# Linear attention feeding a mixture of experts: q and the decays turned by VectorE in 32x32 blocks, and the next unit's loads put inside the store step

## The chip, the cores and the metric

The kernel runs on one core of one Trainium2 chip. The metric is the time on the device in microseconds (us) from the first to the last instruction of an execution and what lies around it, as the median of several runs.

## The reference

Attention with a decaying state runs first; its output y, with the heads of a token side by side, is the input x of a mixture of 8 experts whose weights P come from a Sinkhorn iteration over the logits.

```
def _attn_ref(q, k, v, alpha):            # each (B=4, H=8, S=768, D=48), float32
    state = zeros((B, H, D, D))
    for t in range(S):
        state = alpha[:, :, t, :, None] * state + einsum('bhd,bhe->bhde', k[:, :, t], v[:, :, t])
        y[:, :, t] = einsum('bhd,bhde->bhe', q[:, :, t], state)
...
def _moe_ref(x, w_gate, w1, w2):          # x (3072, 384), w1 (8, 384, 1024), w2 (8, 1024, 384)
    logits = x @ w_gate
    P = exp(logits - logits.max())
    for _ in range(8):
        P /= P.sum(1, keepdims=True) + 1e-09
        P /= P.sum(0, keepdims=True) + 1e-09
        P *= N / E
    for e in range(E):
        out += P[:, e:e+1] * (maximum(x @ w1[e], 0) @ w2[e])
```

## The kernel before

The tokens are worked in twelve **units** of 256 tokens, three for each of the four batches, numbered 0 to 11 through all batches (`g`). A unit has two **chunks** of 128 tokens. Units 0 and 1 take another path (`direct_chunk`); units 2 to 11 go through three generators that an order written out by hand (`START`, then `UNIT` repeated for each unit) advances step by step, mixed with steps `f` that emit tiles of the first three experts. The order of the instructions on each engine is the order in which these steps emit them; nothing is reordered at run time.

- `attn_block` (steps `b`, sixteen for a unit) loads q, k and alpha of the unit as `qt`, `kt`, `al`, with 16 tokens of a head in each of 128 partitions, and multiplies decays into them and takes the products within 16 tokens: GpSimd makes the products `tmp`, VectorE sums them into the score table `AB`. The first `tmp` of a unit multiplies `qt` by `kt`. The three tiles have one buffer each, so that a unit's loads come after the stores of the unit before.
- The last step of `attn_block`, the **store step**, writes kt, qt, the block decays (`ds`) and the scores (`As`) to DRAM and reads them back in other layouts: `KN` and `QN` with a token in each partition and the heads beside each other, `DN` for the decays, `an` for the scores, `VN` for v straight from the input. For units from 3 on (`g >= TAB`) it also writes decays to `dsw` and reads them back as `win`. All are issued on SP's queue, in the order of the code.
- `attn_decays` (step `d`) turns `DN` with four transposes on TensorE (`psd`) and makes small tables of decays.
- `attn_chunk` (steps `c`) turns k and q of a chunk with four transposes each on TensorE (`psk`, `psq`); ScalarE copies them out of PSUM as `Tk` and `Tq`; VectorE multiplies decays in (`decq`, `deck`), GpSimd one of them (`deck`) and then `A`, which spreads `an` over a 128x128 mask. TensorE makes the scores (`psl`) and the output (`psy`), `attn_tail` adds the state.

Expert tiles write `ps` in PSUM, in four banks; ScalarE reads them as `h` (Relu) or as `r`, VectorE takes the low part of `h`, and a bank is free after that. `r` is stored to DRAM as `raw` on SP's queue.

Engines issue in order: an instruction that waits holds up all that stand behind it on its engine, and a DMA that waits holds up SP's queue.

Of the kernel before, what the change touches and what calls it, by code (L numbers as in the profile page):

```python
# [25 lines left out]
def tile_gla_moe(ctx: ExitStack, tc: tile.TileContext, q, k, v, alpha, wg, w1, w2, out):  # L26
# [126 lines left out]
    def quarter(j):  # L153
        return slice(32 * j, 32 * j + 32)
# [134 lines left out]
    KN = [ap1.tile([P, NCH, H, DP], F32, name=f"KN{i}") for i in range(2)]  # L289
    DN = [ap1.tile([16, H, DP], F32, name="DN")] * 2  # L290
    VW = DP + D
# [7 lines left out]

    for x in DN[:1] + ST:  # L300
        GE.memset(x, 0.0)
# [26 lines left out]
    for i in range(NLV):  # L328
        L = 1 << i

        r = sm.tile([P, 16], F32, tag="oddr", name=f"oddr_{i}")
        VE.tensor_reduce(r[:, :16 // L], same.rearrange("p (n z t) -> p n z t", z=2, t=L)[:, :, 0],
                         axis=AX.X, op=ALU.add)
        VE.tensor_copy(odd[:, i].rearrange("p (n t) -> p n t", t=L),
                       r[:, :16 // L].unsqueeze(2).to_broadcast([P, 16 // L, L]))

    def load_v(x, b, t0, Q=SP):
# [3 lines left out]
    def direct_chunk(ch, got):  # L341
# [140 lines left out]
        yield from attn_tail(0, ch, vn[:, c], K_, Q_, A, Dl[:, :, 0])  # L482

    def attn_block(b, u, got):

# [3 lines left out]
        vec = VE  # L489
        src = lambda x: x[b, :, t0:t0 + U].rearrange("h (n t) d -> n h (t d)", t=16)  # L490
        qt, kt, al = (ap1.tile([P, 16, D], F32, tag=x, name=f"{x}_{nm}") for x in ("qt", "kt", "al"))
        for x, y in ((qt, q), (al, alpha), (kt, k)):
            (GE if lop[0] else SP).dma_start(x, src(y))
        if TAB <= g < TAB + 2:
# [50 lines left out]
        if True:  # L545

            t = mult(pool, "tmp4", [16], Af[:, 0:256:17], qt, kt)
            yield
            total(*t)
            yield  # L550
            vec.tensor_mul(qt, qt, al)
            for L in (1, 2, 4, 8):
                todo, merge = level(L)
                for x in todo:
                    t = mult(pool if lop[0] else x[0], *x[1:])
                    yield
# [9 lines left out]
        As = dr.tile([H, U, 16], F32, tag="As", name=f"As_{nm}")  # L566
        qn, kn, dn = QN[g % 2], KN[g % 2], DN[g % 2]
        vn = VN[g % 2]
        an = ap2.tile([P, NCH, H, 16], F32, tag="an", name=f"an_{nm}")
        def put(t, t_):  # L570
            for x, y in ((ks, ko), (qs, qo)):
                dma(x[:, t:t_].rearrange("h (n t) d -> n h (t d)", t=16), y[t // 2:t_ // 2])

        put(0, U)
        dma(ds.rearrange("h n d -> n h d"), al[:, 0])
        for c in range(NCH) if g >= TAB else ():
            dma(dsw[g % 2][:, c, :8].rearrange("h n d -> n h d"), al[c * 64:c * 64 + 64, 0])
        if True:
            dma(As.rearrange("h (n s) t -> n h (s t)", s=16), Af)
        for c in range(NCH):  # L580
            sl = slice(c * P, (c + 1) * P)
            dma(kn[:, c, :, :D], ks[:, sl].rearrange("h t d -> t h d"))
            dma(qn[:, c, :, :D], qs[:, sl].rearrange("h t d -> t h d"))
            if c == 0:
                dma(dn[:, :, :D], ds.rearrange("h n d -> n h d"))
            dma(an[:, c], As[:, sl].rearrange("h p t -> p h t"))
            load_v(vn[:, c], b, t0 + c * P)
        if g >= TAB:
            win = ap1.tile([P, 7, D], F32, tag="tmp2", name=f"win_{nm}")
            for c in range(NCH):  # L590
                e = dsw[g % 2][0, c, 1]
                dma(win[c * 64:c * 64 + 64], bass.AP(tensor=e.tensor, offset=e.offset,
                                                     ap=[[D, 8], [NCH * 15 * D, H], [1, 7 * D]]))
            got["win"] = win
        got.update(qn=qn, kn=kn, dn=dn, vn=vn, an=an)
        yield

    def attn_decays(b, u, got):

        nm = f"{b}_{u}"  # L600
        dn = got["dn"]
        psd = psa.tile([P, 512], F32, tag="psa", name=f"psd_{nm}")
        for j in range(NP):
            tr(psd[:, j * 16:(j + 1) * 16], dn[:, 2 * j:2 * j + 2].rearrange("p h d -> p (h d)"), ident[:16, :16])
        dT = ap2.tile([P, NCH, NP, 2, 4], F32, tag="dT", name=f"dT_{nm}")
        VE.tensor_copy(dT.rearrange("p c j z n -> p c j (z n)"),
                              psd[:, :NP * 16].rearrange("p (j c n) -> p c j n", c=NCH, n=8))

# [32 lines left out]
    def attn_chunk(b, ch, got):  # L641
# [5 lines left out]
        nm = f"{b}_{ch}"  # L647
        T2 = []
        for s in "kq":
            ps = psa.tile([P, 512], F32, tag="psa", name=f"ps{s}_{nm}")  # L650
            for j in range(NP):
# [22 lines left out]
        for L, tq, tk in ((32, got["q32"][:, c].rearrange("p j z b -> p (j z) b"),  # L674
# [832 lines left out]
```

## Time and profile before

| | |
|---|---|
| time, median of 3 runs | 1646.62 us (1645.75 to 1653.32) |
| the profiled execution's own time | 1645.72 us |
| its span, first to last instruction | 1643.8 us |
| TensorE (PE) busy | 1591.0 us, 97% of the span |
| VectorE (DVE) busy | 1262.3 us, 77% |
| ScalarE (ACT) busy | 916.5 us, 56% |
| GpSimd (POOL) busy | 390.9 us, 24% |
| attention and first experts | to about 735 us |

An engine's busy time is the sum over its instructions; a row of a timeline gives the start, the busy time, the instructions merged in it, and in brackets the idle time before them with what ended it. PE is TensorE's matmuls, SPq SyncE's DMA queue.

### The profile page before, as it was taken

Reading aid. Unit: us, or ns where it says so; the run is one execution under the profiler, and the core shown is the slowest. Engines: PE = TensorE matmul, PEld = TensorE weight load, DVE = VectorE, ACT = ScalarE, POOL = GpSimd, SP = SyncE. Lnnn points to the kernel's source line nnn. Section 1 sums busy time; section 2 is a strip of 40 time slices with the busy share of each in tenths; the row PEclk is TensorE's granted clock in tenths of the full one; section 3 lists DMA queues with packets and bytes.
Section 4 is the critical chain, followed back from the end, with each engine's and each line's share of the span. In section 5 each row is a group of like instructions: output and inputs, shape, how many; then the busy total and the mean of one; then the engine's idle time right before and its main releaser. Section 6 shows DMA issues by size and latency. Waiting matters only on the chain.

```text
span 1643.8 us, 50626 instructions
## 1 busy us (share of the span) xinstructions
PE 1591.0 (97%) x21760; PEld 1399.8 (85%) x21760; DVE 1262.3 (77%) x2693; ACT 916.5 (56%) x2106; POOL 390.9 (24%) x395
## 2 busy tenths in 40 slices
PE   5689999999999999999999999999999999999998
PEld 4567777777777777777899999999999999999998
DVE  5887776665666565367798988898888888899998
ACT  3655533333333333355777766666666676765554
POOL 5457544643644462175000000000000000000000
PEclk9799999999999999999999999999999999999999
DMA  7463243144134323120412131213121322213332
GB/s 165 103 139 105 67 116 93 53 125 110 57 89 116 81 69 89 42 79 30 107 50 88 60 98 59 97 60 88 55 92 59 88 69 88 67 62 117 113 121 88
DMA packets 180072, 141.92 MB, mean 86 GB/s; under 512 B 112232, under 2 KB 169832, under 8 KB 179848
## 3 DMA queue, kind: packets, MB, share of 16 engines
q1 hardware_dynamic: 178104, 131.99, 29.0%
q0 software_dynamic: 1744, 6.70, 1.6%
q8 instruction: 170, 2.79, 0.7%
q14 instruction: 54, 0.44, 0.1%
HBM read 91.00 MB, written 47.65 MB: 84 GB/s over the span
## 4 chain that ended last, share of the span: by engine, by line
PE 87%; DVE 4%; DMA 1%; SPq 1%; ACT 1%; issue 1%; POOL 0%; DVEq 0%; ACTq 0%; POOLq 0%
PE ps L67 30%; PE p1a L67 17%; PE p2x L67 14%; PE p1b L67 10%; PE p2y L67 7%; PE p2v L67 4%; PE psl L67 2%; PE psy L67 2%; SPq L58 1%; DVE h L58 1%; DVE w L58 1%; PE psk L70 1%; DVE acc L58 1%; PE psq L70 1%; PE pss L67 0%
## 5 line engine op out<-in xcount | busy, mean ns | idle before, releaser
L67 PEld LDWEIGHTS <-h 128*128 128x128 f16 x6684 | 570.5, 98 | 105.2 <-issue 2.5
L67 PEld LDWEIGHTS <-w 128*128 128x128 f16 x6984 | 565.3, 98 | 58.1 <-issue 12.4
L67 PE MATMUL ps<-xT,w 128*128 128x256 f16 (+1 forms) x2664 | 301.2, 272 | 8.6 <-DVE h L58 6.4
L67 PE MATMUL ps<-w,h 128*128 128x384 f16 x1728 | 299.3, 326 | 0.8 <-DVE h L58 0.7
L58 DVE TENSOR_TENSOR h<-hf,h 128x256 f16<-128x256 f32 x472 | 279.0, 618 | 23.6 <-ACT h L58 23.6
L67 PE MATMUL p2x<-w,h 128*128 128x192 f16 x2820 | 270.7, 246 | 0.0
L58 ACT CAST h<-hf 128x256 f16<-128x256 f32 x472 | 249.5, 567 | 9.3 <-DVE hf L58 4.5
L58 DVE TENSOR_TENSOR hf<-hf 128x256 f32<-128x256 f32 x354 | 181.8, 513 | 39.6 <-ACT hf L58 31.2
L58 ACT ACTIVATE h<-ps 128x256 f16<-128x256 f32 (+1 forms) x296 | 110.5, 377 | 161.5 <-PE ps L67 160.3
L58 POOL TENSOR_TENSOR tmp<-qt,kt 128x768 f32<-128x768 f32 (+2 forms) x87 | 156.2, 1802 | 156.2 <-DVE qt L58 84.6
L58 DVE SCALAR_TENSOR_TENSOR h<-ps,h 128x256 f16<-128x256 f32 (+1 forms) x296 | 117.5, 413 | 96.0 <-ACT h L58 94.7
L67 PE MATMUL p1a<-xT,w 128*128 128x128 f16 (+1 forms) x2160 | 179.1, 237 | 0.0
L67 PE MATMUL p1b<-xT,w 128*128 128x256 f16 (+1 forms) x1440 | 158.0, 246 | 0.0
L58 ACT ACTIVATE hf<-p1b 128x512 f32<-128x512 f32 x118 | 70.3, 596 | 151.4 <-DVE h L58 118.4
L67 PEld LDWEIGHTS <-wx 128*128 128x128 f16 x2160 | 147.4, 98 | 7.9 <-issue 4.9
L67 PE MATMUL p2y<-w,h 128*128 128x192 f16 x1404 | 134.9, 246 | 0.0
L58 DVE TENSOR_REDUCE AB<-tmp 128x16 f32<-128x768 f32 (+2 forms) x90 | 81.4, 904 | 64.1 <-POOL tmp L58 63.7
L67 PE MATMUL p1a<-xc,wx 128*128 128x128 f16 x1440 | 119.5, 219 | 3.6 <-DVE p1b L58 1.6
L58 ACT ACTIVATE hf<-p1a 128x512 f32<-128x512 f32 x118 | 70.4, 597 | 64.7 <-PE p1a L67 64.7
L58 ACT COPY r<-ps 128x384 f32<-128x384 f32 x72 | 34.2, 476 | 102.3 <-PE ps L67 62.3
L58 ACT COPY A<-psl 16x128 f32<-16x128 f32 (+3 forms) x164 | 52.4, 326 | 49.2 <-PE psl L67 47.7
L67 PE MATMUL p2v<-w,h 128*128 128x192 f16 x708 | 68.1, 246 | 0.0
(235 smaller groups left out, 1830.5 us busy)
## 6 DMA issues: line engine op xcount, KB each, us to landing
accd<-acc SPq DMA_DIRECT2D x48, 384.0 KB
acc<-accd SPq DMA_DIRECT2D x48, 384.0 KB
raw<-r SPq DMA_DIRECT2D x72, 192.0 KB
ri<-raw SPq DMA_DIRECT2D x72, 192.0 KB
w1f<-in_moe_w_dram SPq DMA_DIRECT2D x20, 384.0 KB
w2f<-in_moe_w_dram SPq DMA_DIRECT2D x5, 1536.0 KB
VN<-in_v_dram SPq DMA_DIRECT2D x48, 96.0 KB
out_dram<-acc SPq DMA_DIRECT2D x11, 384.0 KB
```

The lines of the kernel that those rows point to most:

```text
L58: r = f(*a, **k_)
L67: tc.keep_in_program_order(nc.tensor.matmul(out_, lhsT, rhs, start=start, stop=stop, **k_))
L70: tc.keep_in_program_order(nc.tensor.transpose(out=out_, in_=in_, identity=idn))
```

## The change

Four things are changed, for the units from 3 on (`turned`); unit 2 keeps the old way, with `DN` in a buffer of `Tq`.

1. q and the decays go to DRAM with the even heads ahead of the odd ones, and come back as `QN` and `DY` in pieces: 32 tokens (or blocks) in 32 partitions, one 32-wide or 16-wide piece of a head's 48 numbers after the other, four DMAs each. VectorE's 32x32 block transpose then gives `Tq` and `dT` directly. The transposes `psq` and `psd` on TensorE and ScalarE's copy of `psq` are gone. k is turned on TensorE as it was.
2. `load_block(g + 1, SP)` loads q, k and alpha of the next unit inside the store step, behind the reads of DY, KN (first chunk) and QN, and ahead of win, an and the second chunk's KN. The first step of `attn_block` then finds them loaded. In units 4 and 5 these loads were issued on GpSimd's queue before.
3. Within the store step the decays are stored first, then k, q and the scores.
4. v is loaded behind: in the second step of `attn_block` where the buffer is free by then, and at the end of the store step otherwise.

```diff
+    DY = ap1.tile([P, NP * 16 // 32, 32], F32, name="DY")
...
+    def in32(x):
+        return x.rearrange("p c h d -> p (c h d)").rearrange("p (s t) -> p s t", t=32)
...
+    loaded = {}
+
+    def load_block(g, eng):
+
+        if g in loaded or g >= len(units):
+            return
+        b, u = units[g]
+        src = lambda x: x[b, :, u * U:(u + 1) * U].rearrange("h (n t) d -> n h (t d)", t=16)
+        loaded[g] = [ap1.tile([P, 16, D], F32, tag=x, name=f"{x}_{b}_{u}") for x in ("qt", "kt", "al")]
+        for x, y in zip(loaded[g], (q, k, alpha)):
+            eng.dma_start(x, src(y))
+
     def attn_block(b, u, got):
 
         g = b * NU + u
         t0 = u * U
         nm = f"{b}_{u}"
         vec = VE
-        src = lambda x: x[b, :, t0:t0 + U].rearrange("h (n t) d -> n h (t d)", t=16)
-        qt, kt, al = (ap1.tile([P, 16, D], F32, tag=x, name=f"{x}_{nm}") for x in ("qt", "kt", "al"))
-        for x, y in ((qt, q), (al, alpha), (kt, k)):
-            (GE if lop[0] else SP).dma_start(x, src(y))
+        load_block(g, GE if lop[0] else SP)
+        qt, kt, al = loaded[g]
+        turned = g >= TAB
+        vn = VN[g % 2]
...
             t = mult(pool, "tmp4", [16], Af[:, 0:256:17], qt, kt)
             yield
+            ahead = turned and all(steps[i] >= XDONE[i] for i in range((g - 2) * NCH, (g - 1) * NCH))
+            for c in range(NCH) if ahead else ():
+                load_v(vn[:, c], b, t0 + c * P)
             total(*t)
             yield
...
-        qn, kn, dn = QN[g % 2], KN[g % 2], DN[g % 2]
-        vn = VN[g % 2]
+        qn, kn = QN[g % 2], KN[g % 2]
         an = ap2.tile([P, NCH, H, 16], F32, tag="an", name=f"an_{nm}")
-        def put(t, t_):
-            for x, y in ((ks, ko), (qs, qo)):
-                dma(x[:, t:t_].rearrange("h (n t) d -> n h (t d)", t=16), y[t // 2:t_ // 2])
-
-        put(0, U)
-        dma(ds.rearrange("h n d -> n h d"), al[:, 0])
-        for c in range(NCH) if g >= TAB else ():
-            dma(dsw[g % 2][:, c, :8].rearrange("h n d -> n h d"), al[c * 64:c * 64 + 64, 0])
-        if True:
-            dma(As.rearrange("h (n s) t -> n h (s t)", s=16), Af)
-        for c in range(NCH):
-            sl = slice(c * P, (c + 1) * P)
-            dma(kn[:, c, :, :D], ks[:, sl].rearrange("h t d -> t h d"))
-            dma(qn[:, c, :, :D], qs[:, sl].rearrange("h t d -> t h d"))
-            if c == 0:
-                dma(dn[:, :, :D], ds.rearrange("h n d -> n h d"))
-            dma(an[:, c], As[:, sl].rearrange("h p t -> p h t"))
-            load_v(vn[:, c], b, t0 + c * P)
-        if g >= TAB:
-            win = ap1.tile([P, 7, D], F32, tag="tmp2", name=f"win_{nm}")
+        dsh = lambda: [dma(dsw[g % 2][:, c, :8].rearrange("h n d -> n h d"), al[c * 64:c * 64 + 64, 0])
+                       for c in range(NCH)]
+        load_an = lambda c: dma(an[:, c], As[:, c * P:(c + 1) * P].rearrange("h p t -> p h t"))
+        def load_win():
+
+            win = got["win"] = ap1.tile([P, 7, D], F32, tag="tmp2", name=f"win_{nm}")
             for c in range(NCH):
                 e = dsw[g % 2][0, c, 1]
                 dma(win[c * 64:c * 64 + 64], bass.AP(tensor=e.tensor, offset=e.offset,
                                                      ap=[[D, 8], [NCH * 15 * D, H], [1, 7 * D]]))
-            got["win"] = win
-        got.update(qn=qn, kn=kn, dn=dn, vn=vn, an=an)
+
+        if turned:
+            heads = lambda x, r: x.rearrange("(r j) t d -> r j t d", r=2)[r]
+            rows = lambda x, r: x.rearrange("(m r) t d -> r m t d", r=2)[r]
+            for r in range(2):
+                dma(heads(ds, r).rearrange("j n d -> n j d"), rows(al, r)[:, 0])
+            dsh()
+            dma(ks.rearrange("h (n t) d -> n h (t d)", t=16), ko)
+            for r in range(2):
+                dma(heads(qs, r).rearrange("j (n t) d -> n j (t d)", t=16), rows(qo, r))
+            dma(As.rearrange("h (n s) t -> n h (s t)", s=16), Af)
+            load_k = lambda c: dma(kn[:, c, :, :D], ks[:, c * P:(c + 1) * P].rearrange("h t d -> t h d"))
+            for x, y in ((DY, ds), (in32(qn), qs)):
+                for i in range(4):
+                    r, z = divmod(i, 2)
+                    w = 32 - 16 * z
+                    dma(x[quarter(i), :, :w], heads(y, r).rearrange("j t d -> (j t) d")
+                        .rearrange("(s t) d -> t s d", t=32)[:, :, 32 * z:32 * z + w])
+                if y is ds:
+                    load_k(0)
+            load_block(g + 1, SP)
+            load_win()
+            load_an(0)
+            load_k(1)
+            load_an(1)
...
+        for c in range(NCH) if turned and not ahead else ():
+            load_v(vn[:, c], b, t0 + c * P)
+        got.update(qn=qn, kn=kn, vn=vn, an=an)
...
-        dn = got["dn"]
-        psd = psa.tile([P, 512], F32, tag="psa", name=f"psd_{nm}")
-        for j in range(NP):
-            tr(psd[:, j * 16:(j + 1) * 16], dn[:, 2 * j:2 * j + 2].rearrange("p h d -> p (h d)"), ident[:16, :16])
+        dn = got.get("dn")
         dT = ap2.tile([P, NCH, NP, 2, 4], F32, tag="dT", name=f"dT_{nm}")
-        VE.tensor_copy(dT.rearrange("p c j z n -> p c j (z n)"),
-                              psd[:, :NP * 16].rearrange("p (j c n) -> p c j n", c=NCH, n=8))
+        if dn is None:
+            VE.transpose(dT.rearrange("p c j z n -> p j c (z n)"), DY.rearrange("p m (j c n) -> p (m j) c n", c=NCH, n=8))
...
+        tabbed = got["k128"] is None
         for s in "kq":
+            if tabbed and s == "q":
+                t = ap2.tile([P, NP, P], F32, tag=f"T{s}", name=f"T{s}_{nm}")
+                y = in32(got["qn"]).rearrange("p (j s) t -> p j (s t)", j=NP)
+                VE.transpose(t, y[:, :, c * P:(c + 1) * P])
+                T2.append(t)
+                continue
```

On SP's queue, the store step of unit 5 stood so before, from the read of the decays on (`DN`, `an` the scores, `VN` v, `win` the windows of decays, `qt`, `al`, `kt` the loads for unit 6, `raw` stores of expert tiles):

```order
L58 DMA DN_120<-ds_1_2_4576 16x8x48
L58 DMA an_1_2_4578<-As_1_2_4577 128x8x16
L58 DMA VN1_124<-in_v_dram 128x4x48 x2
L58 DMA KN1_119<-ks_1_2_4575 128x8x48
L58 DMA QN1_117<-qs_1_2_4574 128x8x48
...
L58 DMA win_1_2_4596<-dsw1_149 64x1x336 x2
L58 DMA qt_2_0_4599<-in_q_dram 128x1x768
L58 DMA al_2_0_4601<-in_alpha_dram 128x1x768
L58 DMA kt_2_0_4600<-in_k_dram 128x1x768
L58 DMA raw0_104<-r_0_6_4649 128x384
```

The same place in the changed kernel:

```order
L58 DMA KN1_119<-ks_1_2_4565 128x8x48
L58 DMA QN1_117<-qs_1_2_4564 32x32x32
L58 DMA QN1_117<-qs_1_2_4564 32x32x16
...
L58 DMA qt_2_0_4586<-in_q_dram 128x1x768
L58 DMA kt_2_0_4587<-in_k_dram 128x1x768
L58 DMA al_2_0_4588<-in_alpha_dram 128x1x768
L58 DMA win_1_2_4592<-dsw1_149 64x1x336 x2
L58 DMA an_1_2_4568<-As_1_2_4567 128x8x16
L58 DMA KN1_119<-ks_1_2_4565 128x8x48
L58 DMA an_1_2_4568<-As_1_2_4567 128x8x16
L58 DMA raw0_104<-r_0_6_4637 128x384
```

The loads for unit 6 moved ahead of `win`, of both halves of `an` and of the second chunk's `KN`; v is gone from the step.

On VectorE, unit 4's first chunk before (`dT` the turned decays, `AB` the sum over unit 5's first product `tmp`, `decq` and `deck` the products on the turned q and k):

```order
L58 COPY dT_1_1_3745<-psd_1_1_3740 128x64
L58 TENSOR_TENSOR e2_1_1_3747<-dT_1_1_3745 128x32
...
L58 TENSOR_REDUCE AB1_126<-tmp4_1_2_30_3738 128x16
L58 TENSOR_TENSOR decq32_1_2_3779<-Tq_1_2_3777,q32_0_133 128x256
L58 TENSOR_TENSOR deck32_1_2_3781<-Tk_1_2_3770,k32_0_135 128x256
L58 TENSOR_TENSOR decq64_1_2_3783<-Tq_1_2_3777,pre_0_129 128x256
```

and now:

```order
L58 STREAM_TRANSPOSE dT_1_1_3741<-DY_120 128x4x2x8
L58 TENSOR_TENSOR e2_1_1_3743<-dT_1_1_3741 128x32
...
L58 TENSOR_REDUCE AB1_126<-tmp4_1_2_30_3739 128x16
L58 STREAM_TRANSPOSE Tq_1_2_3772<-QN0_116 128x512
L58 TENSOR_TENSOR decq32_1_2_3774<-Tq_1_2_3772,q32_0_133 128x256
L58 TENSOR_TENSOR deck32_1_2_3776<-Tk_1_2_3770,k32_0_135 128x256
L58 TENSOR_TENSOR decq64_1_2_3778<-Tq_1_2_3772,pre_0_129 128x256
```

The two transposes stand where the copy out of PSUM and the first use of ScalarE's copy stood; nothing else moved on VectorE. In the other units from 3 on but this one, `AB` stands behind `decq`, `deck` and `win`.

On GpSimd's queue, unit 5's first chunk and the first product of unit 6 stand as before; the rows are those of the changed kernel:

```order
L58 TENSOR_TENSOR ST0_121<-ST1_122,dtot_1_1_3745 48x4x48 x2
...
L58 TENSOR_TENSOR deck64_1_4_4662<-Tk_1_4_4652,suf_1_132 128x256
L58 TENSOR_TENSOR A_1_4_4664<-an_1_2_4568,mask_71 128x8x8x16
L58 TENSOR_TENSOR tmp4_2_0_39_4709<-qt_2_0_4586,kt_2_0_4587 128x768
L58 TENSOR_TENSOR tmp1_2_0_40_4743<-qt_2_0_4586,kt_2_0_4587 128x384
```

`A` reads `an` and stands ahead of the first `tmp`, which reads `qt` and `kt`; that did not move. Only in unit 4 the first `tmp` stands ahead of `deck` and `A`, before and now.

## Rows read from the trace of the kernel before

**Rows 1.** The page, part 1: busy time and share of the span.

```profile
PE 1591.0 (97%) x21760; PEld 1399.8 (85%) x21760; DVE 1262.3 (77%) x2693; ACT 916.5 (56%) x2106; POOL 390.9 (24%) x395
```

**Rows 2.** Windows: us, busy by engine (instructions), PE's granted clock, DMA share, GB/s.

```profile
260.00:669.00 409.00, 408.08 (x5428) 310.71 (x5425) 253.95 (x519) 151.92 (x418) 196.03 (x145) 1.00 0.35 88
```

**Rows 3.** Timeline of PE in unit 10: start, us, engine, line, operation.

```profile
573.15 0.42 PE L70 MATMUL psd<-ident,DN 16*128 16x16 f32 x4
573.50 3.10 PE L67 MATMUL ps<-w,h 128*128 128x384 f16 x18
576.44 0.60 PE L70 MATMUL psk<-ident,KN 128*128 128x128 f32 x4
576.88 0.60 PE L70 MATMUL psq<-ident,QN 128*128 128x128 f32 x4
577.31 2.11 PE L67 MATMUL ps<-w,h 128*128 128x384 f16 x12
```

**Rows 4.** Timeline of VectorE in unit 10.

```profile
578.18 0.51 DVE L58 TENSOR_TENSOR decq<-Tq,q 128x256 f32<-128x256 f32 x1 [2.36 <-ACT Tq L58]
```

**Rows 5.** Timeline of SP's queue in the store step of unit 10.

```profile
560.75 0.58 SPq L58 DMA_DIRECT2D ks<-kt  x1
...
564.84 0.54 SPq L58 DMA_DIRECT2D As<-AB  x1
565.48 0.53 SPq L58 DMA_DIRECT2D KN<-ks  x1
...
575.38 0.58 SPq L58 DMA_DIRECT2D qt<-in_q_dram  x1
```

**Rows 6.** Timeline of GpSimd in unit 10.

```profile
578.37 2.08 POOL L58 TENSOR_TENSOR A<-an,mask 128x1024 f32<-128x1024 f32 x1
582.42 1.81 POOL L58 TENSOR_TENSOR tmp<-qt,kt 128x768 f32<-128x768 f32 x1 [1.97 <-DMA kt<-in_k_dram]
```

**Rows 7.** Timeline of SP's queue in unit 7.

```profile
386.28 0.60 SPq L58 DMA_DIRECT2D ks<-kt  x1
...
401.19 0.57 SPq L58 DMA_DIRECT2D qt<-in_q_dram  x1
...
407.10 0.79 SPq L58 DMA_DIRECT2D td<-win  x1
410.52 0.61 SPq L58 DMA_DIRECT2D kb<-td  x1
```

**Rows 8.** Timeline of GpSimd in unit 7.

```profile
409.42 1.80 POOL L58 TENSOR_TENSOR tmp<-qt,kt 128x768 f32<-128x768 f32 x1 [3.79 <-DMA kt<-in_k_dram]
```

**Rows 9.** Timeline of VectorE in unit 7.

```profile
411.26 0.95 DVE L58 TENSOR_REDUCE AB<-tmp 128x16 f32<-128x768 f32 x1 [2.48 <-POOL tmp L58]
```

**Rows 10.** Timeline of PE in unit 7.

```profile
401.62 0.60 PE L70 MATMUL psk<-ident,KN 128*128 128x128 f32 x4
...
412.60 2.34 PE L67 MATMUL ps<-xT,w 128*128 128x256 f16 x18 [0.77 <-DVE h L58]
```

**Rows 11.** Timeline of SP's queue in unit 3.

```profile
151.98 0.93 SPq L58 DMA_DIRECT2D ks<-kt  x1
```

**Rows 12.** Timeline of GpSimd in unit 3.

```profile
152.99 0.28 POOL L58 TENSOR_TENSOR al<-al 128x48 f32<-128x48 f32 x1
...
169.95 1.87 POOL L58 TENSOR_TENSOR tmp<-qt,kt 128x768 f32<-128x768 f32 x1
```

**Rows 13.** Timeline of VectorE in unit 3.

```profile
174.90 0.95 DVE L58 TENSOR_REDUCE AB<-tmp 128x16 f32<-128x768 f32 x1
```

**Rows 14.** Timeline of PE in unit 3.

```profile
178.03 1.14 PE L67 MATMUL ps<-xT,w 128*128 128x256 f16 x9 [1.75 <-DVE h L58]
```

**Rows 15.** Timeline of SP's queue in unit 4.

```profile
213.07 0.58 SPq L58 DMA_DIRECT2D ks<-kt  x1
```

**Rows 16.** Timeline of GpSimd in unit 4.

```profile
229.00 1.81 POOL L58 TENSOR_TENSOR tmp<-qt,kt 128x768 f32<-128x768 f32 x1 [7.16 <-DMA kt<-in_k_dram]
```

**Rows 17.** Timeline of VectorE in unit 4.

```profile
230.84 0.95 DVE L58 TENSOR_REDUCE AB<-tmp 128x16 f32<-128x768 f32 x1 [2.85 <-POOL tmp L58]
```

More of the change, by code (lines that the diff above doesn't have):

```diff
@@ L289, in tile_gla_moe @@
     KN = [ap1.tile([P, NCH, H, DP], F32, name=f"KN{i}") for i in range(2)]
-    DN = [ap1.tile([16, H, DP], F32, name="DN")] * 2
+    DY = ap1.tile([P, NP * 16 // 32, 32], F32, name="DY")
     VW = DP + D
@@ L298, in tile_gla_moe @@
                           for x, n in (("pre", 4), ("suf", 4), ("q32", 2), ("k32", 2)))
-    for x in DN[:1] + ST:
+    for x in [DY] + ST:
         GE.memset(x, 0.0)
@@ L593, in attn_block @@
                                                      ap=[[D, 8], [NCH * 15 * D, H], [1, 7 * D]]))
-            got["win"] = win
-        got.update(qn=qn, kn=kn, dn=dn, vn=vn, an=an)
+        if turned:
[22 more added lines that the diff above has]
+            load_an(1)
+        else:
+            dn = ap2.tile([P, H, DP], F32, tag="Tq", name="DN")[:16]
+            GE.memset(dn[:, :, D:], 0.0)
+            for x, y in ((ks, ko), (qs, qo)):
+                dma(x.rearrange("h (n t) d -> n h (t d)", t=16), y)
+            dma(ds.rearrange("h n d -> n h d"), al[:, 0])
+            dma(As.rearrange("h (n s) t -> n h (s t)", s=16), Af)
+            for c in range(NCH):
+                sl = slice(c * P, (c + 1) * P)
+                dma(kn[:, c, :, :D], ks[:, sl].rearrange("h t d -> t h d"))
+                dma(qn[:, c, :, :D], qs[:, sl].rearrange("h t d -> t h d"))
+                if c == 0:
+                    dma(dn[:, :, :D], ds.rearrange("h n d -> n h d"))
+                load_an(c)
+                load_v(vn[:, c], b, t0 + c * P)
+            got["dn"] = dn
+        for c in range(NCH) if turned and not ahead else ():
+            load_v(vn[:, c], b, t0 + c * P)
+        got.update(qn=qn, kn=kn, vn=vn, an=an)
         yield
@@ L600, in attn_decays @@
         nm = f"{b}_{u}"
-        dn = got["dn"]
-        psd = psa.tile([P, 512], F32, tag="psa", name=f"psd_{nm}")
-        for j in range(NP):
-            tr(psd[:, j * 16:(j + 1) * 16], dn[:, 2 * j:2 * j + 2].rearrange("p h d -> p (h d)"), ident[:16, :16])
+        dn = got.get("dn")
         dT = ap2.tile([P, NCH, NP, 2, 4], F32, tag="dT", name=f"dT_{nm}")
-        VE.tensor_copy(dT.rearrange("p c j z n -> p c j (z n)"),
-                              psd[:, :NP * 16].rearrange("p (j c n) -> p c j n", c=NCH, n=8))
+        if dn is None:
+            VE.transpose(dT.rearrange("p c j z n -> p j c (z n)"), DY.rearrange("p m (j c n) -> p (m j) c n", c=NCH, n=8))
+        else:
+            psd = psa.tile([P, 512], F32, tag="psa", name=f"psd_{nm}")
+            for j in range(NP):
+                tr(psd[:, j * 16:(j + 1) * 16], dn[:, 2 * j:2 * j + 2].rearrange("p h d -> p (h d)"), ident[:16, :16])
+            VE.tensor_copy(dT.rearrange("p c j z n -> p c j (z n)"),
+                                  psd[:, :NP * 16].rearrange("p (j c n) -> p c j n", c=NCH, n=8))
         g2 = (b * NU + u) % 2
@@ L682, in attn_chunk @@
                              mask.unsqueeze(2).unsqueeze(3).to_broadcast([P, 8, H, 16]))
-        tabbed = got["k128"] is None
         kb = None
```

## The prediction

> **What bounds the kernel now.** I read the page first: TensorE is busy for 1591.0 of 1643.8 us [rows 1]. The windows then show that the part which the change touches is no exception: from 260 to 669 us, six units' worth of attention with expert tiles between them, PE is busy 408.08 of 409.00 us at full clock, while VectorE has 253.95 and GpSimd 196.03 [rows 2]. So a matmul taken away there shortens the run by what it took, and a wait added elsewhere costs only once PE runs out of PSUM banks. This profiled execution took 1645.72 us, 1.9 us more than its span and 0.9 us under the median of the three runs; the sum is made on it, and 0.9 us are added at the end. A difference under 0.5% (8.2 us) is about what a measurement here cannot tell from none.
>
> **What is removed.** In PE's timeline of unit 10 the four decay transposes start at 573.15 and the next matmul at 573.50: 0.35 us. The four q transposes start at 576.88 and the next matmul at 577.31: 0.43 us [rows 3]. Nine units are turned, with one decay group and two q groups each: 9 x 0.35 + 18 x 0.43 = 10.9 us of PE. ScalarE also loses 18 copies of q, which PE did not wait for.
>
> **What VectorE gets.** No row shows its transpose. The nearest handles half as many elements, a product of 128x256 in 0.51 us [rows 4]; 128x512 lies between that (no dearer) and 1.02 us, twice that. I take 0.6. It stands where VectorE idled 2.36 us for ScalarE's copy of q [rows 4]; the product after it needs the copy of k anyway. Cost on the path: 0 for the first chunk of a unit, and at most 18 x 0.5 us if VectorE were the bound, which PE's row denies. The decay turn replaces a copy of like size: nothing.
>
> **What the store step now issues.** This is where the gain can go. In unit 10 the step starts at 560.75 and gets to the next unit's q load at 575.38, after 19 DMAs, 0.77 us each; without waits one takes 565.48 - 564.84 = 0.64 us [rows 5]. After the change 17 DMAs stand ahead of that load (decays 2, windows' decays 2, k 1, q 2, scores 1, DY 4, k 1, q 4): 10.9 us at 0.64, 13.1 at 0.77; I take 12.0. So the loads start about 2.6 us earlier than in unit 10. But win and an, the score table that GpSimd's product A reads, now stand *behind* these three loads, where an stood far ahead of them. From the issue of the first load to the first product on kt, its wait over, went 582.42 - 575.38 = 7.0 us in unit 10 [rows 5, 6] and 409.42 - 401.19 = 8.2 in unit 7 [rows 7, 8]. A small transfer does not pass them: in unit 7 td was issued at 407.10 and kb, which waits for it, at 410.52, 1.1 us after the load was in [rows 7, 8]. So an lands 12.0 + 7.6 + 1.0 = 20.6 us after the step's start (18.9 with the short ends and 1.0, 22.3 with the long). In unit 10 A ran at 578.37, 17.6 us after it; it now waits 3 us and ends at 20.6 + 2.1 = 22.7, and the product tmp of the next unit follows it on GpSimd's queue.
>
> **What that wait holds up.** VectorE's reduction AB waits for tmp, and the expert tiles' h stand behind AB. Unit 7 shows the price: tmp came 409.42 - 401.62 = 7.8 us after the k transposes, AB waited 2.48 us for it, and PE stood 0.77 us for h [rows 8, 9, 10]. Hence PE's loss is tmp minus k transposes, less 7.03 us. Without the q transposes between them the allowance is 6.60. Without the decays the k transposes come 0.35 us sooner after the step's start: at 15.34 us for unit 10 (576.44 - 560.75 - 0.35) and 14.99 for unit 7 (401.62 - 386.28 - 0.35) [rows 3, 5, 7, 10]. Loss: 22.7 - 15.34 - 6.60 = 0.8 us, and 1.1. For the six units 5 to 10 I take 0.94 each, 5.6 us, of which unit 7 pays 0.77 already: 4.9 net. Unit 11 loads nothing more and loses nothing.
>
> Unit 3 pays more. Its step starts with al, whose last product ends at 153.27, 1.3 us after k was stored at 151.98 [rows 11, 12]. So an lands at 153.27 + 20.6 = 173.9; A ends at 176.0 and tmp (1.87 us) at 177.8. Before, AB began at 174.90 and PE resumed at 178.03 after 1.75 us of idling [rows 12, 13, 14]. AB is 2.9 us later, and PE arrives 0.8 us earlier (decays and one q group): 3.7 us more idling.
>
> In unit 4 tmp comes before A and needs kt only. Before, it was issued on GpSimd's queue and started at 229.00, 15.9 us after the step's start at 213.07, with AB waiting 2.85 us [rows 15, 16, 17]. Now kt is the second of the loads: issued at 12.6, landing by about 5.8 us later (in unit 10, 582.42 less that load's issue, two pitches after 575.38), at 18.4. AB is 2.5 us later; between 0 and 3.3 us reach PE (the rest of its bank slack, or all of it with the 0.8); I take 1.4.
>
> **The sum.** -10.9 + 4.9 + 3.7 + 1.4 = -0.9 us: span 1643, run 1644.8, median about 1646. The earlier kt and the v loads moved behind are worth nothing by themselves, since A now ends last on GpSimd.
>
> **Small pieces.** Between the first k read (565.48) and the q load (575.38) the queue moved some 8,400 pieces (k and q 4096 of 192 B, v 2048, an 2048 of 64 B, the rest small) in 9.9 us [rows 5]: 1.18 ns a piece, if pieces are the limit. The q read now has 4096 pieces of 128 and 64 B instead of 2048 of 192 B. Between DY and the loads stand 256 + 1024 + 4096 pieces, 6.3 us by this price, and nine DMAs, 5.8 to 6.9 us by issue. They come out even, so the sum leaves the issue's number. The Trainium skill ("DMA: Bandwidth & Descriptors", § Why small descriptors are slow) speaks against the change: a fixed overhead of about 3 cycles per packet beside one cycle for every 32 bytes. By it a head's token costs (4 + 3) + (2 + 3) = 12 cycles in two pieces instead of 9 in one, so that q's read would take a third longer; that is an estimate from the page, no row here shows 128-byte pieces, and by it my sum would rise a little, as in the second rival.
>
> **Rivals.**
> *The loads do not delay an* (the issue runs at 0.64 us and the loads take 7.0, or small transfers slip between the large). At an = 18.9 A ends at 21.0: units 5 to 10 lose nothing, unit 7's 0.77 goes, unit 3 loses 2.0: 1645.7 - 10.9 - 0.8 + 2.0 = 1636, and 1632 if unit 3's 1.75 goes as well. For it: before the change an landed in time everywhere. Against: td in unit 7. Chance 0.24.
> *Slower: the queue is late with q's small pieces.* Place: the four q reads, ahead of the loads. If pieces bound, the reads end 6.3 us after their first packet, about 1.2 us after the loads could start, and every us there is paid in units 3 to 10, eight times: 1646 + 9.6 = 1656. It decides from about 1.1 us of extra lateness, an landing after 21.7. At the long ends (22.3) it is 1646 + 13 = 1659. For it: 4096 pieces in one go, on 32 partitions each. Against: the 1.18 ns already holds 2048 pieces of 64 bytes. Chance 0.21. The rule of the Trainium skill on small descriptors, above, is this rival's mechanism.
> *VectorE is late.* If a turn takes 2 us beside GpSimd, 18 x 1.4 us go to VectorE, of which the first chunks' half is covered by the wait on the copy; the rest delays h by 1.4 us in nine places, inside most of PE's allowance: about 1650. Chance 0.05.
> That the change doesn't do what it says: the loads are inside the store step, but A sits ahead of the first product that needs them, so no unit starts sooner; this is in the forecast.
>
> **How the numbers follow.** The forecast (waits about as large as the matmuls saved) has 0.50, its own range 1639 to 1654. With the late VectorE, which is also inside 0.5%, no change has 0.55; faster is the first rival, 0.24, and slower the second, 0.21. The range reaches to 1636.5 and 1657, the two rivals' times, which leaves about 2 in 10 outside.
>
> **What would show it.** Right: no psd and q transposes after 150 us on PE; GpSimd's A waits for a DMA in units 3 and 5 to 10, by about 3 us; its wait for kt is gone; AB waits longer for tmp, and PE shows gaps of about 1 us some 10 us after each unit's k transposes, the largest (5 us) near 180. Wrong: A starts right behind deck (first rival), or A waits 5 us (second), or VectorE's transposes wait for QN.

## The result and the profile after

The changed kernel takes 1671.57 us (median of 4 runs, 1669.72 to 1677.18) beside 1646.85 for the kernel before: a ratio of 1.0148, with a 95% interval of 1.0111 to 1.0184. It is slower by about 24.7 us; the forecast was no change, and the time lies outside the range. The profiled execution has a span of 1668.0 us, 24.2 more than before.

The first part of the page, the windows from 270 to 690 us (the stretch that answers to [rows 2], as far as the shift lets it) and the waits of PE between 100 and 760 us (in all, times, longest):

```profile
PE 1591.9 (95%) x21652; PEld 1396.1 (84%) x21652; DVE 1286.8 (77%) x2711; ACT 908.5 (54%) x2088; POOL 387.0 (23%) x390
```

```profile
270.00:690.00 420.00, 401.48 (x5216) 303.41 (x5214) 274.84 (x530) 145.01 (x403) 195.61 (x145) 0.98 0.36 84
```

```profile
PE ps L67 <- DVE h L58: 28.5, 10, 5.5
```

Two things are to be seen. The 108 transposes are gone (21760 to 21652 instructions), but PE is as long busy as before (1591.9 against 1591.0), so the other matmuls took some 11.8 us more: 10.9 for the missing ones and 0.9. And PE stood 28.5 us for `h`, in ten places, where before it stood 3.2 us in three. The balance is 25.3 more of waits for `h`, 11.8 of slower matmuls, less 10.9 removed, less 2.0 of smaller differences elsewhere (the remainder): 24.2.

Unit 10 shows how one of the ten places comes about. SP's queue, GpSimd, VectorE and PE (`lg` is the sum over the gate's products, and stands ahead of the first `h`):

```profile
582.11 1.22 SPq L58 DMA_DIRECT2D ds<-al  x2
...
594.36 0.80 SPq L58 DMA_DIRECT2D qt<-in_q_dram  x1
595.21 0.60 SPq L58 DMA_DIRECT2D kt<-in_k_dram  x1
595.85 0.60 SPq L58 DMA_DIRECT2D al<-in_alpha_dram  x1
596.49 1.23 SPq L58 DMA_DIRECT2D win<-dsw  x2
597.76 0.45 SPq L58 DMA_DIRECT2D an<-As  x1
```

```profile
603.67 1.90 POOL L58 TENSOR_TENSOR A<-an,mask 128x1024 f32<-128x1024 f32 x1 [4.22 <-DMA an<-As]
605.52 1.80 POOL L58 TENSOR_TENSOR tmp<-qt,kt 128x768 f32<-128x768 f32 x1
```

```profile
596.77 0.71 DVE L58 STREAM_TRANSPOSE Tq<-QN 128x512 f32<-128x512 f32 x1 [0.58 <-DMA QN<-qs]
597.51 0.43 DVE L58 TENSOR_TENSOR decq<-Tq,q 128x256 f32<-128x256 f32 x1
598.54 0.43 DVE L58 TENSOR_TENSOR deck<-Tk,k 128x256 f32<-128x256 f32 x1 [0.60 <-ACT Tk L58]
598.88 0.84 DVE L58 TENSOR_TENSOR decq<-Tq,pre 128x256 f32<-128x256 f32 x1
603.42 4.21 DVE L58 TENSOR_TENSOR win<-win 128x144 f32<-128x144 f32 x4 [3.69 <-DMA win<-dsw]
607.66 0.18 DVE L58 TENSOR_REDUCE lg<-psg 128x9 f32<-128x18 f32 x1
607.76 0.41 DVE L58 SCALAR_TENSOR_TENSOR h<-ps,h 128x256 f16<-128x256 f32 x1
...
608.84 0.94 DVE L58 TENSOR_REDUCE AB<-tmp 128x16 f32<-128x768 f32 x1
```

```profile
597.29 0.60 PE L70 MATMUL psk<-ident,KN 128*128 128x128 f32 x4
...
608.23 5.76 PE L67 MATMUL ps<-xT,w 128*128 128x256 f16 x36 [4.11 <-DVE h L58]
```

`an` lands 603.67 - 582.11 = 21.6 us after the step's start; 20.6 was forecast. `AB`, which was to hold up `h`, waits for nothing. Three `h` stand ahead of it, and what holds these up is `win`: VectorE waits 3.69 us for it and then needs 4.21 us for the four small products on it. Two of the four take 1.87 and 1.84 us, about as long as `A` (1.90) and `tmp` (1.80), which run beside them. Before, the four had taken 0.90 us in this unit, with no wait ahead of them:

```profile
580.99 0.90 DVE L58 TENSOR_TENSOR win<-win 128x144 f32<-128x144 f32 x4
```

In units 3 and 5 to 10, the seven whose gap follows this pattern, the four took 4.13 to 4.29 us. Both the wait for `win` and that for `an` run through all units (VectorE's and GpSimd's waits, 100 to 760 us; before, `win` was waited for once, 2.0 us, and `an` never):

```profile
DVE win L58 <- DMA win<-dsw: 23.2, 7, 4.9
```

```profile
POOL A L58 <- DMA an<-As: 27.7, 7, 6.0
```

PE's clock is the other part. Windows of 4 us from each of the eight larger gaps' ends, units 3 to 10 (the seventh column is the granted clock):

```profile
182.00:186.00 4.00, 4.00 (x125) 2.98 (x125) 3.49 (x9) 0.46 (x2) 3.11 (x4) 0.61 0.30 102
244.00:248.00 4.00, 3.78 (x18) 2.46 (x17) 3.50 (x9) 0.38 (x1) 2.84 (x4) 0.50 0.57 155
306.00:310.00 4.00, 3.46 (x31) 2.96 (x31) 3.88 (x9) 0.93 (x3) 1.57 (x2) 1.00 0.33 86
366.00:370.00 4.00, 3.92 (x22) 2.80 (x22) 3.56 (x9) 0.51 (x2) 1.43 (x2) 0.57 0.17 55
427.00:431.00 4.00, 3.74 (x20) 2.72 (x19) 3.55 (x8) 0.39 (x1) 1.25 (x2) 0.57 0.20 59
488.00:492.00 4.00, 4.00 (x24) 2.98 (x24) 3.48 (x9) 0.77 (x2) 1.45 (x2) 0.61 0.19 59
548.00:552.00 4.00, 3.95 (x37) 3.54 (x37) 3.55 (x9) 1.15 (x3) 1.04 (x2) 1.00 0.17 55
608.00:612.00 4.00, 3.77 (x20) 2.75 (x20) 3.31 (x8) 0.39 (x1) 0.95 (x1) 0.57 0.18 55
```

Behind six of the eight gaps PE ran most of the next 4 us at the lower level (1.2 GHz), with 39 to 50% of a window's work lost. By these shares the six windows lost 10.3 us (an estimate), most of the 11.8. From 260 to 669 us before, the granted clock was 1.00 throughout [rows 2].

### The profile page after: what moved, and what is told of

The parts are those of the page before. It is cut to its first block, busy times and chain, and to the rows that moved or that the text cites. A ratio compares the mean times of both kernels' runs of the same rounds, so it can differ in the third digit from the quotient of the medians.

```text
span 1668.0 us, 50479 instructions
## 1 busy us (share of the span) xinstructions
PE 1591.9 (95%) x21652; PEld 1396.1 (84%) x21652; DVE 1286.8 (77%) x2711; ACT 908.5 (54%) x2088; POOL 387.0 (23%) x390
## 4 chain that ended last, share of the span: by engine, by line
PE 72%; DVE 8%; SPq 6%; DMA 3%; POOL 3%; issue 1%; ACT 1%; DVEq 0%; ACTq 0%
PE ps L67 20%; PE p1a L67 16%; PE p2x L67 13%; PE p1b L67 9%; PE p2y L67 7%; SPq L58 6%; PE p2v L67 4%; DMA win<-dsw 3%; POOL tmp L58 2%; DVE win L58 2%; PE psl L67 2%; DVE AB L58 1%; PE psy L67 1%; DVE h L58 1%; DVE w L58 1%
## 5 line engine op out<-in xcount | busy, mean ns | idle before, releaser
L67 PE MATMUL ps<-xT,w 128*128 128x256 f16 (+1 forms) x2664 | 310.8, 277 | 33.1 <-DVE h L58 31.0
```

The source lines that it names most:

```text
L67: tc.keep_in_program_order(nc.tensor.matmul(out_, lhsT, rhs, start=start, stop=stop, **k_))
```

## The experiments

Each ratio is to runs of the kernel before on the same chip, whose median was 1646.85 us for the changed kernel and lay between 1648.0 and 1649.9 us for the others.

| run | median us | ratio (95%) |
|---|---|---|
| the changed kernel | 1671.6 | 1.0148 (1.0111 to 1.0184) |
| e1 loads last | 1652.4 | 1.0028 (1.0018 to 1.0038) |
| e2 `win` ahead of the loads | 1662.4 | 1.0087 (1.0062 to 1.0111) |
| e3 `an` ahead of the loads | 1647.9 | 0.9995 (0.9982 to 1.0007) |
| e4 before, loads 10th in the step | 1646.4 | 0.9986 (0.9974 to 0.9997) |
| e5 products on `win` later | 1666.5 | 1.0120 (1.0093 to 1.0147) |
| e6 turning alone | 1653.5 | 1.0024 (1.0014 to 1.0034) |
| e8 loads on GpSimd's queue | 1682.3 | 1.0202 (1.0183 to 1.0222) |
| e9 before, loads 18th in the step | 1669.3 | 1.0136 (1.0108 to 1.0165) |
| e10 `an`, `win` ahead, unit 4's loads early | 1643.5 | 0.9961 (0.9946 to 0.9976) |
| e11 `an` ahead, unit 4's loads early | 1647.8 | 0.9991 (0.9980 to 1.0001) |
| e13 loads last, unit 4's early | 1649.9 | 1.0000 (0.9987 to 1.0013) |
| e14 unit 4's loads early alone | 1672.5 | 1.0131 (1.0115 to 1.0147) |
| e15 before, `an`, `win`, then the loads | 1652.7 | 1.0023 (1.0008 to 1.0037) |
| e17 `an`, `win` ahead | 1646.7 | 0.9979 (0.9968 to 0.9990) |
| e20 as e17, from unit 5 on | 1638.7 | 0.9942 (0.9924 to 0.9959) |

Four theories are named in the expectations. W: `win` is late behind the loads, and VectorE's products on it hold up `h`. A: `an` is late, and through `A`, `tmp` and `AB` it holds up `h`, as the prediction had it. T: the turning itself costs. P, formed after the first four runs: the place of the loads costs.

**Which of the two late reads costs.** The changed kernel's order is the three loads, `win`, `an(0)`, `KN`, `an(1)`. e1, e2 and e3 move the loads alone:

```diff
 e1            e2            e3
+load_win()   +load_win()   +load_an(0)
+load_an(0)    load_block    load_block
+load_k(1)     load_an(0)    load_win()
+load_an(1)    load_k(1)     load_k(1)
 load_block    load_an(1)    load_an(1)
```

> The changed kernel with the next unit's three loads moved to the end of the store step, behind win, an and KN. Theory W (win is late behind the loads, VectorE's four products on it stand ahead of h, PE runs dry): VectorE's wait for win, 23.2 us in the changed kernel, falls under 3 us, PE's gaps of 2.3 to 5.5 us in units 3 to 10 go, and the saved matmuls show: 1646.9 - 10.9 + about 2 of unit 2 = 1637 us, 1633 to 1642. Theory A (an alone is late, GpSimd's product A and tmp hold up AB): the same, since an also passes the loads. Theory T (the turning itself costs, small pieces on the queue or transposes on VectorE): the time stays above 1660 us.

> The changed kernel with win alone ahead of the three loads; an stays behind them. Theory W: VectorE's wait for win goes, PE's gaps shrink to what a late tmp costs, about 1 us in units 5 to 10 and 1 to 4 us in units 3 and 4: 1644 to 1652 us, and GpSimd still waits some 4 us for an. Theory A: GpSimd's wait for an is what counts, nothing is gained, 1665 us or more. Theory T: above 1660 us.

> The changed kernel with the first half of an ahead of the loads, win still behind them. If win at VectorE is what holds up h (theory W): GpSimd's product A runs early, VectorE still waits 3 us and more for win in seven units, 1660 to 1675 us. If an at GpSimd is (theory A): 1640 to 1652 us.

All three expectations of theory W missed their numbers; e3 fell into theory A's range, e1 and e2 into neither's. e1 won back 1.2% of the 1.5%, not all of it. (In its profiled execution, which took 1680 us, GpSimd's first `tmp` in unit 4 waited 16 us for kt, which now came last.) e2 won back 0.6%: VectorE's wait for `win` is gone, but GpSimd still waits for `an`, and now `AB` waits for `tmp`, 82.4 us from 100 to 760 us against 56.1 in the changed kernel. Unit 10 of e2, VectorE and PE:

```profile
602.22 0.95 DVE L58 TENSOR_REDUCE AB<-tmp 128x16 f32<-128x768 f32 x1 [2.73 <-POOL tmp L58]
```

```profile
603.56 1.14 PE L67 MATMUL ps<-xT,w 128*128 128x256 f16 x9 [1.02 <-DVE h L58]
```

This is the path of theory A by itself. It cost 1.02 us here, 0.84 more in the unit's second chunk, and 10.2 us in units 5 to 10, where the changed kernel lost 18.5. e3 won back nearly everything, with `win` as late as before. Its unit 10, VectorE, GpSimd and PE:

```profile
586.60 0.91 DVE L58 TENSOR_TENSOR win<-win 128x144 f32<-128x144 f32 x4 [3.47 <-DMA win<-dsw]
587.54 0.18 DVE L58 TENSOR_REDUCE lg<-psg 128x9 f32<-128x18 f32 x1
587.63 0.41 DVE L58 SCALAR_TENSOR_TENSOR h<-ps,h 128x256 f16<-128x256 f32 x1
```

```profile
582.81 2.08 POOL L58 TENSOR_TENSOR A<-an,mask 128x1024 f32<-128x1024 f32 x1
584.85 1.80 POOL L58 TENSOR_TENSOR tmp<-qt,kt 128x768 f32<-128x768 f32 x1
```

```profile
588.10 4.09 PE L67 MATMUL ps<-xT,w 128*128 128x256 f16 x36 [0.58 <-DVE h L58]
```

VectorE waits 3.47 us for `win` here as there (3.69), but the four products then take 0.91 us and not 4.21, and PE loses 0.58 and not 4.11. What differs is GpSimd: `A` and `tmp` are over by 586.65, while in the changed kernel both ran beside the products, released by the same late transfers. So the wait for `win` alone nearly fits into PE's slack (from 100 to 760 us VectorE waits 26.4 us for it in e3, and 23.2 in the changed kernel); the wait with products of 4.21 us behind it does not. The Trainium skill ("SBUF — State Buffer", § Who interferes with whom) says that a VectorE instruction with two inputs in SBUF contends with a GpSimd instruction that reads SBUF, over ports that it calls an exclusive lock. The traces agree: a product on 128x48 elements took 0.21 us alone and 1.73 to 1.95 us beside `A` or `tmp`, about one instruction of GpSimd.

e3 brings `A`, `tmp` and `AB` forward together, so that it does not separate the collision from the late `tmp`. That the collision held PE in the changed kernel is read from the rows: there `AB` waits for nothing, and the `h` behind the four products are what PE waited for.

**VectorE's program instead of the queue.** e5 leaves the DMAs of the store step as they are and puts the products on `win` one step later, behind several `h` (the store `td` and the read `kb`, which follow from them, come later too).

```diff
-        if tabbed and not c:
-            win = got["win"]
-            VE.tensor_mul(win[:, 0:3], win[:, 0:3], win[:, 3:6])
...
         yield
         if tabbed and not c:
+            win = got["win"]
+            VE.tensor_mul(win[:, 0:3], win[:, 0:3], win[:, 3:6])
...
             td = got["td"] = ...
```

> The changed kernel with VectorE's four products on win emitted one step later, behind several h (win gets a buffer of its own for that); the order of the DMAs is untouched. Theory W: h no longer stands behind win, so that most of the loss goes though win lands as late as before: 1643 to 1654 us. Theory A: no gain, 1665 us or more. Theory T: above 1660 us.

Its 1.0120 beside the changed kernel's 1.0148 is hardly a gain, as the intervals overlap; it lies in theory A's range. In unit 10, behind the first three `h`, VectorE's next row now reads

```profile
600.75 0.95 DVE L58 TENSOR_REDUCE AB<-tmp 128x16 f32<-128x768 f32 x1 [2.98 <-POOL tmp L58]
```

and PE still stood 24.2 us for `h`, in twelve places. Two chains were late by nearly as much, `win` with its products and `an`-`A`-`tmp`-`AB`; to repair one uncovers the other. That is also why e2 and e3 do not add up to e17.

**The loads without the turning.** e4 and e9 are the kernel before, q and decays still turned on TensorE, with the loads put inside the store step ahead of `win` and `an`: behind nine DMAs in e4, behind 17 in e9. e15 is e9 with `an(0)` and `win` ahead of the loads.

```diff
 # e4, in the loop over the chunks
+                if c == 0 and g >= TAB:
+                    load_block(g + 1, SP)
+                    load_win()
             dma(an[:, c], ...)
 # e9, behind the loop, which now reads KN in halves, QN, DN and VN alone
+        if g >= TAB:
+            load_block(g + 1, SP)
+            load_win()
+        for c in range(NCH):
+            dma(an[:, c], ...)
```

> The kernel before, q and decays still turned on TensorE, with only the three loads put inside the store step, ahead of win, an and the second chunk's reads. Theories W and A: the loss without the saving, some 23 us of idle PE and 10 us of lower clock on top of 1646.9: 1670 to 1685 us, with PE gaps of 2 to 5 us in units 3 to 10. Theory T: no loss from the loads, 1640 to 1652 us.

> The kernel before, q and decays still turned on TensorE, with the three loads in the store step as its 18th DMA, as in the changed kernel (both chunks' reads of k in two halves, q and v ahead of them), and win and an behind. Against the run in which they stood 10th and cost nothing this moves the loads alone. Theory P: win and an land some 5 us later than there, VectorE waits for win, PE shows gaps of 2 to 5 us in units 3 to 10: 1665 to 1685 us. Theory T: 1643 to 1652 us, since nothing is turned.

> The kernel before with the loads put behind 17 DMAs of the store step, as in the run that took 1669, but with the first half of an and win ahead of them (the loads then come as the 21st DMA). If win and an behind the loads are the cause: PE's gaps in units 5 to 10 go, 1646 to 1654 us, what is left being units 3 and 4, where kt comes late. If the late loads by themselves are: 1665 us or more.

e4 cost nothing, against the expectation of both W and A. With the loads at the tenth place `win` and `an` are behind them too, but in time: PE's waits for `h` fell to 1.5 us. e9, eight places later, lost as much as the changed kernel, with nothing turned, and by the same waits (VectorE, GpSimd and PE, 100 to 760 us; the profiled execution took 1681):

```profile
DVE win L58 <- DMA win<-dsw: 16.9, 6, 4.9
```

```profile
POOL A L58 <- DMA an<-As: 30.0, 9, 6.1
```

```profile
PE ps L67 <- DVE h L58: 21.3, 9, 4.6
```

In unit 10 the four products on `win` took 4.17 us here too, beside `A` and `tmp`. e15 put `an(0)` and `win` ahead of the loads, and 1.1 of the 1.4% went, as its expectation had it; its largest gap is 4.49 us in unit 4, where kt is wanted first. What costs most is therefore not that the loads are late, nor that something stands behind them, but both together: transfers needed at a given time stand behind three long ones that start too late to be over by then. e9 also gives a comparison for q's small pieces. In its unit 10 the loads were issued 602.69 - 590.85 = 11.8 us after the step's start, and `A` ran 8.9 us after that; in the changed kernel 12.3 and 9.3:

```profile
590.85 0.58 SPq L58 DMA_DIRECT2D ks<-kt  x1
...
602.69 0.62 SPq L58 DMA_DIRECT2D qt<-in_q_dram  x1
```

```profile
611.60 1.90 POOL L58 TENSOR_TENSOR A<-an,mask 128x1024 f32<-128x1024 f32 x1 [3.09 <-DMA an<-As]
```

Behind 17 DMAs with q's small pieces the loads were thus issued 0.4 us later than behind 17 with whole rows, and `A` came another 0.4 us later. e9's 17 hold v and the second half of k in place of the pieces, so that this compares two mixes and does not price the pieces by themselves.

**The turning without the loads.** e6 takes `load_block(g + 1, SP)` out of the store step (the loads are issued in the next unit's first step, for units 3 to 5 on GpSimd's queue); e8 issues them in the store step, but on GpSimd's queue.

```diff
 # e6                              # e8
-            load_block(g + 1, SP)  -            load_block(g + 1, SP)
                                    +            load_block(g + 1, GE)
```

> The changed kernel without the loads in the store step: they are issued in the next unit's first step, as before the change (units 3 to 5 on GpSimd's queue, the later ones on SP's, behind win, an and KN). Theory P (the place of the loads costs: behind 17 DMAs, ahead of win and an in units 5 to 10, and off GpSimd's queue in unit 4): PE's gaps in units 4 to 10 go, the one of unit 3 stays near 2 us, and the saved matmuls show in full: 1648 - 10.9 = 1637 us, 1634 to 1641. Theory T (the turning costs about what it saves, by its small pieces and eight more DMAs): 1645 to 1655 us.

> The changed kernel with the three loads of the store step issued on GpSimd's DMA queue, where the engine is idle for some 15 us. Theory P: win and an no longer queue behind the loads, so that VectorE's waits for win fall from 23 us to a few, and 1636 to 1645 us if the loads do not slow the small reads; if the loads take the small reads' share of the DMA engines, KN and QN come some 3 us later and the time is 1645 to 1660. Theory T: 1645 us or more.

Both missed theory P's numbers, and both lie where theory T had them; but T does not explain e9, which loses as much with nothing turned, nor the last versions below. In e6 units 3 and 4 kept gaps of 5.04 and 4.12 us: the loads on GpSimd's queue now run while q's pieces are read, and VectorE, which turns q itself, waits for these pieces (unit 3):

```profile
175.73 0.71 DVE L58 STREAM_TRANSPOSE Tq<-QN 128x512 f32<-128x512 f32 x1 [4.80 <-DMA QN<-qs]
```

In e8 VectorE waits so in nine places, 46.2 us in all, and it is the slowest run of all. A second queue does not take the loads out of the way: in unit 10, while these loads and the reads of q are both under way, the 16 DMA engines show no idle share (1.08, the column before the last):

```profile
608.00:618.00 10.00, 10.00 (x96) 6.98 (x95) 3.52 (x15) 3.22 (x12) 2.22 (x4) 1.00 1.08 195
```

**Unit 4.** There `AB` and the first `tmp` stand ahead of the turning, so that kt is wanted first. Three runs put that unit's loads ahead of the reads of q:

```diff
                 if y is ds:
                     load_k(0)
+                    if g == 4:
+                        load_block(g + 1, SP)
```

> The changed kernel with one edit: in unit 4 the loads stand ahead of the reads of q. It prices unit 4 in the changed kernel, where PE idles 3.8 us and then runs some 3 us at the lower clock: 1664 to 1668 us if tmp behind its load of k holds that unit, 1670 to 1673 if not.

> As the run with an alone ahead of the loads (win behind them), and in unit 4 the loads ahead of the reads of q. This moves unit 4 alone against that run: its gap of 3.8 us and the low clock behind it go, 1640 to 1646 us; if unit 4's gap comes from VectorE or from q read late it stays, 1646 to 1650 us.

> The changed kernel with the loads last in the store step, except in unit 4, where they stand ahead of the reads of q. The run with loads last in all units had no gap over 0.6 us in units 5 to 10 and 7.5 us in unit 4, and took 1652 us. Theory P: unit 4's gap falls by 4 to 6 us and some 3 us of low clock with it: 1639 to 1646 us. Theory T: 1650 us or more.

e14 and e11 gained nothing clear of noise over the changed kernel and e3. In e11 VectorE and PE show why: `tmp` comes sooner, but now q is late, and the product on it collides with `A`:

```profile
233.99 0.95 DVE L58 TENSOR_REDUCE AB<-tmp 128x16 f32<-128x768 f32 x1 [2.68 <-POOL tmp L58]
237.10 0.71 DVE L58 STREAM_TRANSPOSE Tq<-QN 128x512 f32<-128x512 f32 x1 [2.15 <-DMA QN<-qs]
237.85 2.04 DVE L58 TENSOR_TENSOR decq<-Tq,q 128x256 f32<-128x256 f32 x1
```

```profile
242.76 2.61 PE L67 MATMUL ps<-xT,w 128*128 128x256 f16 x13 [3.72 <-DVE h L58]
```

e13 gained 0.3% over e1, less than expected, with a gap of 3.99 us left in unit 4.

**Versions that beat both kernels.** e17 has `load_an(0)`, `load_win()`, then the loads; e10 is the same with unit 4's loads early. e20 is e17 with the turning and the moved loads only from unit 5 on; units 2 to 4 go the old way.

```diff
-        turned = g >= TAB
+        turned = g >= TAB + 2
...
+            load_an(0)
+            load_win()
             load_block(g + 1, SP)
-            load_win()
-            load_an(0)
             load_k(1)
             load_an(1)
```

> The changed kernel with the first half of an and win ahead of the three loads, and in unit 4 alone the loads ahead of the reads of q (there VectorE sums the next unit's first tmp before it turns q). Theory P (place of the loads): both chains that fed PE's gaps in units 5 to 10 are in time, no gap over 0.5 us there; unit 4's gap of 3.8 us falls to under 2; unit 3 keeps about 2 us: 1636 to 1645 us, some 4 us under the run with an alone ahead. Theory T (the turning eats what it saves): 1646 us or more.

> The changed kernel with the first half of an and win ahead of the loads in every unit, and the loads behind the reads of q in unit 4 too. If putting the loads ahead of q in unit 4 was worth nothing there, as two runs say, 1642 to 1645 us, the same as with it; if kt's load decides unit 4, 1645 to 1650.

> The same order (an, win, then the loads), but the turning by VectorE and the moved loads only from unit 5 on; units 3 and 4 go as before the change, with the loads for units 4 and 5 on GpSimd's queue. If units 3 and 4 are what is left of the loss (gaps of 2.8 and 3.9 us and some 3 us of low clock in the best run so far, less 2.4 us of matmuls saved there): 5 to 7 us under that run, or about 1649 - 7 x 1.2 = 1640 us, ratio 0.993 to 0.996. If their cost only moves on to unit 5: ratio 0.996 to 1.000.

The times expected of e10 and e20 came in; e17 came in by its second case. e17 differs from the changed kernel in the place of `an(0)` and `win` alone, so that this order is worth 1.7%; the moved loads of v and the new order of the stores are in both and are not the cause. e10 and e17 are faster than before by 0.4 and 0.2%; their intervals overlap, and whether unit 4's early loads are worth something in this order stays open (unit 4's gap was 3.94 us with them and 6.40 without). e20 is faster by 0.6% (0.4 to 0.8), 9.6 us; 7 x 1.21 = 8.5 were to be saved in seven units. Its windows of units 3 and 4 and of 270 to 690 us:

```profile
150.00:210.00 60.00, 58.44 (x833) 44.78 (x832) 43.66 (x78) 28.78 (x72) 35.44 (x29) 1.00 0.37 90
210.00:270.00 60.00, 58.34 (x737) 44.02 (x735) 40.64 (x83) 22.16 (x63) 28.47 (x23) 1.00 0.41 96
270.00:690.00 420.00, 418.94 (x5501) 318.15 (x5498) 276.05 (x551) 152.37 (x423) 193.96 (x145) 1.00 0.36 86
```

PE is busy 418.94 of 420 us where the changed kernel had 401.48, and the clock is 1.00. Turning and moved loads together save about what the turning was priced at, once what waits behind the loads is in time.

## Why the prediction was wrong

| term | forecast us | measured us |
|---|---|---|
| matmuls removed | -10.9 | 108 instructions gone; e20 saved 9.6 (6.8 to 12.5) where seven units were to give 8.5 |
| VectorE's turning of q | 0.6 each | 0.70 to 0.71 each; in unit 10 `deck` behind it still waits 0.60 for the copy of k |
| loads issued after the step's start | 12.0 | 12.3 (unit 10) |
| `an` landed | 20.6 | 21.6 (unit 10); 20.1 to 21.6 in units 3 to 10 |
| units 5 to 10 | 4.9 net | 18.5 of gaps, less 0.77 of before: 17.7 |
| unit 3 | 3.7 | 5.52 - 1.75 = 3.8 |
| unit 4 | 1.4 | 3.8; PE had not waited for `h` there before |
| lower clock | not in the sum | 11.8 |

The forecast was no change, and the kernel became 1.5% slower. The queue was read rightly: the place of the loads, their time, that small transfers do not pass them, and which unit pays most by its idle time. The step that failed is the one from the late `an` to PE, "PE's loss is tmp minus k transposes, less 7.03 us", with 0.94 us for each of units 5 to 10. By that step unit 10 should have lost 605.52 - 597.29 - 6.60 = 1.6 us with the measured times; it lost 4.11. The path that it follows is real, but it is the smaller part: e2, where `an` alone is late, lost 10.2 us in units 5 to 10, against 5.6 forecast and 18.5 in the changed kernel. The text named `win` as standing behind the loads and then followed `an` alone. VectorE's program has the products on `win` ahead of the `h` that PE needs, and `AB` only behind three of them, so that `win`'s lateness reaches PE first. And four products that took 0.90 us were left out: made to run at the same time as `A` and `tmp`, they took 4.21. In e3, which leaves the wait for `win` and takes away the late `A` and `tmp`, they took 0.91 us and PE lost 0.58.

Unit 3's 3.8 us for a forecast of 3.7 is luck in part: the products on `win` ended last there too, but only 0.3 us after `tmp` (178.95 against 178.65).

The second omission is the clock. Each gap was priced at its idle time; six of the eight were followed by matmuls mostly at half speed, and slower matmuls cost 11.8 us in all, about what the transposes saved. In unit 4 the working took 1.4 from a range of 0 to 3.3 on the strength of a slack in PSUM banks. The first `h` behind the products came 243.75 - 230.84 = 12.9 us after the k transposes, where it had come 235.97 - 226.88 = 9.1 us after them, and PE lost 3.80 us, all of it: there was no slack, and the upper end was the better value.

Of the rivals, the one on the slower side had the right sign by another mechanism: the loads were issued 12.3 us after the step's start in unit 10, where 12.0 was forecast without it, and `an` came before the 21.7 us from which that rival was to decide in each of units 3 to 10. Whether small pieces cost more than whole rows, as the Trainium skill ("DMA: Bandwidth & Descriptors", § Why small descriptors are slow) has it, no run here shows by itself. The first rival, that the loads do not delay `an`, falls by the 27.7 us of waits for it. The late VectorE falls as it was put, since no turn took more than 0.71 us; but VectorE was late beside GpSimd, in the products on `win`.

## What to carry to other kernels

When a long transfer is put earlier in a queue, list everything that stands behind it, and follow each to its first consumer and to what is queued behind that consumer: the costliest is the one whose consumer stands ahead of the bounding engine's feed, not the one that is latest. Ask as well what the late transfers release together, since instructions of two engines that used to be apart can then collide. And where TensorE has no slack, a gap of a few us is to be priced above its idle time, by rows at the lower clock; slack that no row shows is not to be counted on, as unit 4 had none.

## What was not expected of the hardware

A VectorE product on 128x48 elements took 0.21 us alone and up to 1.95 us beside GpSimd's products; one on 128x144 took 0.31 and up to 2.02. PE ran at the lower level behind six of eight gaps of 2.3 to 5.5 us, and at full clock behind two of 2.28 and 2.78 us, while a gap of 2.33 us was followed by a clock of 0.61: the length of the gap alone does not tell which. Loads on GpSimd's queue did not leave SP's small reads alone: VectorE waited up to 7.7 us for q's pieces (e8). Between equal programs up to unit 2 the profiled executions differ by up to some 4 us before 150 us.
